# Soft-MoE attention kernel on one core: slot products on 64x32 tiles, compact key-value products, one bank for a pair's logits, a new order for phase 1

## The chip, the cores and the metric

One core of a Trainium2 chip runs the whole program in one launch. The metric is the device time of that launch in microseconds (us). The kernel before took 251.25 us, the median of 3 runs (250.69 to 259.25).

Engines are named as in the profile: PE (TensorE) multiplies matrices, and PEld is its loading of weights; DVE (VectorE) and ACT (ScalarE) do elementwise work and copy results out of PE's accumulator banks; POOL (GpSimd) does elementwise work on the memory the other engines share; SP (SyncE) issues the large transfers. Each engine works through its own list in order and waits for the others by semaphores.

## The reference: what is computed

Three stages follow one another. The program fuses them.

```python
# 1: attention, 8 batches x 8 heads x 576 positions x 64
q_s = softmax(q, over the 64)            # per position
k_s = softmax(k, over the 576 positions) # per column
kv  = einsum('bhsd,bhse->bhde', k_s, v)  # 64 x 64 per head
x   = einsum('bhsd,bhde->bhse', q_s, kv) # then 4608 tokens x 512
# 2: soft mixture of experts, 8 experts x 4 slots
logits = x @ phi                         # 4608 x 32
d = softmax(logits, over tokens);  slot_input = d.T @ x      # 32 x 512
slot_out = relu(slot_input[e] @ w1[e]) @ w2[e]               # 512 -> 1024 -> 512
y = softmax(logits, over slots) @ slot_out
# 3: top-1 mixture of experts on y, 8 experts, with gates
```

## The kernel before, in words

**Phase 1** covers stage 1 and the slot inputs of stage 2, and x is never formed. A unit u (0 to 7) is two batches (b = 0, 1) and four of their eight heads: 128 partitions by 2304 numbers each of q, of k and of v. Two units with the same batches make a pair (pr, 0 to 3). For each unit the steps are:

- `load_k`, `load_v`, `load_q` put transfers on SP's queue. `k_max` (DVE) and `k_exp` (ACT) make the exponentials of k; `k_t` transposes them on PE, four 128x128 blocks into one bank, and `k_te` copies the bank out (tile `ek`). `k_prod` (L256) multiplies them with v in 64x64 tiles of PE into the tile `kv`.
- `k_norm` copies `kv` into `kvbd`, a tile in which two 64x64 products stand as a block diagonal of a 128x128 block, the rest being zero. `k_kvT` (L287) transposes four such blocks, `k_kvTe` copies them out (ACT), `k_m` (L300) multiplies each with 32 columns of phi, and `k_mt` (DVE) scales the result: `mq`, which takes a position's 64 exponentials of q straight to its 32 logits.
- `q_max` (DVE), `q_sub` (POOL), `q_exp` (ACT), `q_sum` (DVE), `q_mul` (POOL) make the softmax of q (`eq`); `q_t` (L365) transposes it on PE and `q_te` copies it out (`eT`).
- `logits` (L385) multiplies `eT` by `mq` on 128x32 tiles, into two banks per pair, one for each b.

For each pair, `logits_cp`, `logits_t` and the `disp_` steps subtract a running maximum over the tokens and exponentiate the logits into `dz`. `slots_u` (L476) then forms sum over positions of dz times eq, nine matmuls of 256 columns per unit, each on one of two 128x64 tiles of PE (the even and the odd r); `dz` is held with zeros where position group and slot column belong to different b. `slots_e` copies the result out, `slots_t` (L493) adds the two tiles' parts and transposes, `slots_m` scales, `slots_p` (L511) multiplies by `kvbd`, and `slots_acc` adds it to the running slot inputs `acc`.

A matrix product of 32-bit numbers shows as two records each in the trace, a transpose as one. So nine matmuls of `slots_u` are 18 records.

**The order** of phase 1 is written out: a table `ORDER` of some 800 steps, replayed as the program is recorded, so that each engine's list has the table's order. `PAUSES` adds, behind some steps, matmuls on zeros (L605) that nobody reads. Three banks are shared in turn by all results named `tp` (transposes and small products), two by `kv`, two by `L`, one by `U`.

**The weights** of stage 2 (w1 and w2, 33.5 MB) come in 1 MB tiles. `load_w` 0 and 1 have buffers of their own and stand in `ORDER`; the next 19 take over buffers of phase 1 as those are released (`W_TAGS` names them), and eleven more (`W_NEXT`) go into the buffers of weights that were already used, each after its product on PE (L689, `expert_in`). Then come the second product (L733) and a tail of some 74 us that routes the tokens and writes the output; the change leaves it alone.

SP's transfers use eight completion semaphores in turn, shared with the first transfers that ACT issues (`phi`, and the two halves of `wgo`): the ninth transfer waits until the first has landed.

## Time and profile before

| | us |
|---|---|
| median of 3 runs | 251.25 (250.69 to 259.25) |
| the profiled execution, its own time | 250.71 |
| its span, first to last instruction | 248.8 |
| PE busy in the span | 216.6 (87%) |
| DVE, ACT, POOL busy | 152.2, 137.8, 92.7 |
| data moved by the transfers | 76.64 MB, 308 GB/s on average |

The span is 1.9 us shorter than the execution's time; what lies around it is the launch. Busy times are averages over stages with different limits, so they are read by stage: phase 1 ends near 140 us, the experts' weights are through at 175 us, and the tail ends the span.

### The profile page before, as it was taken

How to read it: one execution, taken by the hardware profiler on the slowest of the kernel's cores; microseconds unless marked ns; L12 is line 12 of the kernel's file. 1: busy time of each engine (PE TensorE's matmuls, PEld its weight loads, DVE VectorE, ACT ScalarE, POOL GpSimd, SP SyncE). 2: the span in 40 equal slices, each digit the busy share in tenths (PEclk: the TensorE clock that was granted, in tenths of full speed). 3: DMA queues.
4: the chain of work that ended last, by engine and by line, in shares of the span. 5: the costliest groups of instructions: out<-in, count | busy, mean ns of one | idle time of the engine just before them, and what ended most of it. 6: DMA issues, size and time to landing. Idle time of an engine off the chain costs nothing.

```text
span 248.8 us, 7197 instructions
## 1 busy us (share of the span) xinstructions
PE 216.6 (87%) x2976; PEld 154.5 (62%) x2976; DVE 152.2 (61%) x306; ACT 137.8 (55%) x314; POOL 92.7 (37%) x87
## 2 busy tenths in 40 slices
PE   0678789999999999878999899998999999999940
PEld 0557668777787678665966555332675653888830
DVE  2899788869798877662236571411643888756330
ACT  2879588877997968641533111211333285788640
POOL 5088495727944676506100107312001483100000
PEclk9999999999999999999999999999999999999985
DMA  7999998896899995997999989997079020088991
GB/s 240 411 333 412 407 412 329 322 420 258 323 419 406 420 344 182 366 415 277 310 418 354 351 324 420 419 414 317 3 256 391 31 84 1 4 360 353 379 385 52
DMA packets 18134, 76.64 MB, mean 308 GB/s; under 512 B 3376, under 2 KB 5680, under 8 KB 13360
## 3 DMA queue, kind: packets, MB, share of 16 engines
q1 hardware_dynamic: 16352, 75.50, 77.6%
q0 software_dynamic: 160, 0.52, 0.7%
q8 instruction: 25, 0.41, 0.7%
q10 hardware_dynamic: 1584, 0.10, 0.4%
q14 instruction: 13, 0.11, 0.1%
HBM read 66.68 MB, written 9.44 MB: 306 GB/s over the span
## 4 chain that ended last, share of the span: by engine, by line
PE 57%; DMA 24%; DVE 7%; ACT 4%; issue 3%; SPq 0%; POOL 0%; ACTq 0%; DVEq 0%
DMA vz<-in_moe_w_dram 9%; PE kv L256 6%; PE tp L365 6%; DMA wgo<-n_moe_w_output_gate_dram 6%; PE U L476 6%; PE tp L230 5%; DMA we<-in_moe_w_dram 5%; PE L L385 5%; PE kv L1520 4%; DMA qh<-in_q_dram 4%; PE L L1520 3%; PE U L1520 2%; PE kv L689 2%; PE tp L300 2%; PE tp L287 1%
## 5 line engine op out<-in xcount | busy, mean ns | idle before, releaser
L358 POOL TENSOR_TENSOR eq<-eq,qs 128x1280 f32<-128x1280 f32 (+1 forms) x16 | 33.6, 2117 | 30.5 <-DVE qs L354 30.5
L333 POOL TENSOR_TENSOR eq<-qh,qm 128x1280 f32<-128x1280 f32 (+1 forms) x16 | 33.5, 2116 | 16.9 <-DVE qm L320 15.6
L230 PE MATMUL tp<-ident,kh 128*128 128x128 f32 x144 | 23.7, 299 | 10.7 <-ACT kh L221 9.4
L256 PE MATMUL kv<-vz,ek 64*64 64x64 f32 x1152 | 24.2, 223 | 4.8 <-issue 4.1
L256 PEld LDWEIGHTS kv<-vz,ek 64*64 64x64 f32 x1152 | 20.0, 134 | 9.9 <-issue 8.9
L230 PEld LDWEIGHTS tp<-ident,kh 128*128 128x128 f32 x144 | 17.3, 153 | 14.1 <-issue 8.7
L221 ACT ACTIVATE kh<-kh,nm 128x576 f32<-128x576 f32 x32 | 24.8, 775 | 0.4 <-DVE nm L213 0.2
L213 DVE TENSOR_REDUCE nm<-kh 128x2 f32<-128x1152 f32 x16 | 21.4, 1338 | 4.5 <-DMA kh<-in_k_dram 4.5
L237 ACT COPY eT<-tp 128x512 f32<-128x512 f32 (+1 forms) x32 | 16.4, 534 | 11.5 <-PE tp L365 11.2
L320 DVE TENSOR_REDUCE qm<-qh 128x36 f32<-128x2304 f32 x8 | 20.4, 2545 | 2.6 <-DMA qh<-in_q_dram 2.6
L344 DVE TENSOR_REDUCE qs<-eq 128x20 f32<-128x1280 f32 (+1 forms) x16 | 21.4, 1337 | 0.0
L365 PE MATMUL tp<-ident,eq 128*128 128x128 f32 x144 | 20.8, 280 | 0.3 <-ACT eT L237 0.3
L339 ACT ACTIVATE eq<-eq 128x1280 f32<-128x1280 f32 (+1 forms) x16 | 18.5, 1164 | 1.9 <-POOL eq L333 1.9
L476 PE MATMUL U<-eq,dz 128*64 128x256 f32 x144 | 18.8, 384 | 0.1
L237 ACT COPY ek<-tp 128x512 f32<-128x512 f32 (+1 forms) x32 | 16.4, 534 | 3.6 <-PE tp L230 3.2
L365 PEld LDWEIGHTS tp<-ident,eq 128*128 128x128 f32 x144 | 15.7, 142 | 3.5 <-issue 2.5
L476 PEld LDWEIGHTS U<-eq,dz 128*64 128x64 f32 x144 | 10.9, 136 | 6.0 <-issue 0.7
L733 PE MATMUL U<-we,hte 128*32 128x512 f32 (+1 forms) x118 | 13.4, 572 | 0.9 <-DMA we<-in_moe_w_dram 0.5
L385 PE MATMUL L<-eT,mq 128*32 128x128 f32 (+1 forms) x256 | 11.7, 291 | 0.0
L689 PE MATMUL kv<-we,sTm 128*32 128x256 f32 x188 | 11.6, 381 | 0.1
L1520 PE MATMUL kv<-mst,hr 128*128 128x512 f32 (+1 forms) x32 | 11.3, 390 | 0.0
L859 ACT ACTIVATE ob<-kv,gates 128x512 f32<-128x512 f32 x11 | 7.5, 688 | 4.1 <-PE kv L1520 2.8
(326 smaller groups left out, 415.3 us busy)
## 6 DMA issues: line engine op xcount, KB each, us to landing
we<-in_moe_w_dram SPq DMA_DIRECT2D x24, 1024.0 KB, 8.3
kh<-in_k_dram SPq DMA_DIRECT2D x16, 576.0 KB, 8.9
qh<-in_q_dram SPq DMA_DIRECT2D x8, 1152.0 KB, 9.3
vz<-in_v_dram SPq DMA_DIRECT2D x16, 576.0 KB, 9.4
out_dram<-ob SPq DMA_DIRECT2D x11, 768.0 KB, 3.3
vz<-in_moe_w_dram SPq DMA_DIRECT2D x5, 1024.0 KB, 12.0
vz<-in_moe_w_dram SPq DMA_DIRECT2D x6, 512.0 KB, 6.1
w2q<-in_moe_w_dram SPq DMA_DIRECT2D x4, 512.0 KB, 8.1
```

The costliest lines, as they stand in the source:

```text
L213: nc.vector.tensor_reduce(out=st_["nm", u][:, c], in_=kview(u, c), op=ALU.max, axis=AX.XY, negate=True)
L221: nc.scalar.activation(out=x, in_=x, func=AF.Exp, bias=st_["nm", u][:, c, b:b + 1], accum_out=st_["kz", u][:, c, b:b + 1])
L230: nc.tensor.transpose(tp[:, n * P:(n + 1) * P], ks_[u][:, j * P:(j + 1) * P], ident)
L237: nc.scalar.copy(out=out, in_=in_)
L256: nc.tensor.matmul(kv[b][D * hh:D * hh + D, c * D:(c + 1) * D], ek[a, x], vt[a, x], start=(r == 0), stop=(r == RQ - 1))
L333: nc.gpsimd.tensor_tensor(out=q_part(st_["eq", u], i), in0=q_part(qs_[u], i), in1=q_row(st_["qm", u], i), op=ALU.subtract)
L344: nc.vector.tensor_reduce(out=st_["qs", u][:, QC[i]:QC[i + 1]], in_=q_part(st_["eq", u], i), op=ALU.add, axis=AX.X)
L358: nc.gpsimd.tensor_tensor(out=e, in0=e, in1=q_row(st_["qs", u], i), op=ALU.mult)
L365: nc.tensor.transpose(tp[:, n * P:(n + 1) * P], eq[:, j * P:(j + 1) * P], ident)
L385: nc.tensor.matmul(lg[b][NS * g:NS * g + NS, :n * 64].rearrange("p (i t) -> p i t", t=64), mq[:, 2 * c + b, :], ev[:, c, g:RQ:4, 64 * b:64 ...
L476: nc.tensor.matmul(U[64 * (r % 2):64 * (r % 2) + 64, hf * HH * D:(hf + 1) * HH * D], dz[:, r].rearrange("p b s -> p (b s)"), eq[:, r * HH ...
L1520: nc.tensor.matmul(op, a[:, x], w[:, d0:d1], start=(k == 0), stop=(k == 2))
```

## The change

Six things are changed, all in phase 1 but the last.

1. `slots_u` uses 64x32 tiles, eight of them (two groups b, four places g = r mod 4), so 18 matmuls of 256 columns per unit instead of nine. `dz` loses its zeros and halves in size; the results go to two banks (`L`), copied out by ACT and by DVE, and `slots_t` does eight matmuls instead of four.
2. The block diagonal `kvbd` becomes `kvc`, 64x64 products side by side. `k_norm` copies once instead of twice per b, `k_kvT` transposes two blocks instead of four, `k_m` does eight 64x64 matmuls instead of four of 128x128, into two `tp` banks instead of one, and `k_mt` and `slots_p` follow. `phi` is loaded twice, once for each half of the partitions.
3. The logits of a pair share the one bank `U`; a matmul of zeros opens it.
4. `disp_new` and `disp_al` compute the rescaling factor with other small instructions.
5. `ORDER` and `PAUSES` are new. `load_w.0` moves to the end of phase 1's loads.
6. The two zeroed tiles `sTm` of the expert stage lie in one tile, that of `slots_e`.

```diff
 PAUSES = {
-    "k_te2.0": 1, "q_sub0.1": 32, "load_k1.2": 1, "logits_cp1.3": 3, "logits_out.3": 3, "slots_e.2": 4,
-    "disp_al.3": 3, "slots_m.3": 3, "slots_t.3": 0,
+    "k_te0.0": 2, "k_max0.2": 4, "k_t3.1": 8, "disp_max.3": 5, "logits_out.3": 7, "slots_m.3": 5, "slots_t.3": 0,
 }
...
 ORDER = """
-load_k0.0 k_max0.0 k_exp0.0 k_exp1.0 load_k1.0 load_k0.1 k_max1.0 k_exp2.0 k_t1.0 k_exp3.0 k_t0.0 k_max0.1 load_q.0
...
+load_k0.0 k_max0.0 load_k0.1 k_exp0.0 load_k1.0 k_max0.1 load_q.0 k_exp1.0 k_max1.0 k_exp0.1 k_exp3.0 k_t1.0 k_exp2.0
...
     def k_norm(u, b):
         pr, hf = halves(u)
-        for hh in range(2):
-            a = slice(D * hh, D * hh + D)
-            copy_to(
-                b == 1, kvbd[pr % 2][a, b, 2 * hf:2 * hf + 2, a],
-                st_["kv", u][b][a, :2 * D].rearrange("p (c x) -> p c x", c=2),
-            )
+        copy_to(
+            b == 1, kvc[pr % 2][:, 2 * hf:2 * hf + 2, b, :],
+            st_["kv", u][b][:, :2 * D].rearrange("p (c x) -> p c x", c=2),
+        )
...
     def k_kvT(u):
         for c in range(2):
-            for b in range(2):
-                j = 2 * c + b
-                nc.tensor.transpose(tk[:, j * P:(j + 1) * P], bd[:, b, 2 * hf + c, :], ident)
+            nc.tensor.transpose(
+                tk[:, c * P:(c + 1) * P], kvc[pr % 2][:, 2 * hf + c].rearrange("p b x -> p (b x)"), ident
+            )
...
     def k_m(u):
-        mp = bank("tp")
-        for j in range(4):
-            nc.tensor.matmul(
-                mp[:, NS * j:NS * j + NS], kvT[:, j, :], phi_sb[:, 2 * hf + j // 2, :], start=True, stop=True
-            )
+        mp = [bank("tp") for _ in range(2)]
+        for c in range(2):
+            for hh in range(2):
+                for b in range(2):
+                    a = slice(64 * b, 64 * b + 64)
+                    nc.tensor.matmul(
+                        mp[b][D * hh:D * hh + D, NS * c:NS * c + NS], kvT[a, c, D * hh:D * hh + D],
+                        phi2[a, HH * hf + 2 * c + hh, :], start=True, stop=True,
+                    )
...
     def logits(u):
         if hf == 0:
-            st_["L", pr] = [bank("L") for _ in range(2)]
+            lg = st_["L", pr] = bank("U")
+            nc.tensor.matmul(lg[:, :6 * D], zero[:, :P], zero, start=True, stop=False)
...
     def disp_exp(pr):
-        for b in range(2):
-            nc.scalar.activation(out=dz[64 * b:64 * b + 64, :, b, :], in_=dl[64 * b:64 * b + 64], func=AF.Exp)
+        nc.scalar.activation(out=dz_t[pr % 2], in_=st_.pop(("dl", pr)), func=AF.Exp)
...
     def slots_u(pr, hf):
         for r in range(RQ):
-            nc.tensor.matmul(
-                U[64 * (r % 2):64 * (r % 2) + 64, hf * HH * D:(hf + 1) * HH * D],
-                dz[:, r].rearrange("p b s -> p (b s)"),
-                eq[:, r * HH * D:(r + 1) * HH * D],
-                start=(r < 2),
-                stop=(r >= RQ - 2),
-            )
+            g = r % 4
+            for b in range(2):
+                a = slice(64 * b, 64 * b + 64)
+                nc.tensor.matmul(
+                    U[b][NS * g:NS * g + NS, hf * HH * D:(hf + 1) * HH * D], dz[a, r],
+                    eq[a, r * HH * D:(r + 1) * HH * D], start=(r < 4), stop=(r >= RQ - 4),
+                )
...
-    def slots_e(pr):
-        U_sb = sp.tile([P, H * D], F32, tag="U_sb", name="U_sb")
-        nc.scalar.copy(out=U_sb, in_=st_.pop(("U", pr)))
-        st_["Us", pr] = U_sb
+    def slots_e(pr, b):
+        if b == 0:
+            st_["Us", pr] = sp.tile([P, 2, H * D], F32, tag="U_sb", name="U_sb")
+        copy_to(b == 1, st_["Us", pr][:, b], st_["U", pr][b])
 
     def slots_t(pr):
         for c in range(C):
-            nc.tensor.matmul(tu[:, c * 64:c * 64 + 64], U_sb[:, c * P:(c + 1) * P], sum2, start=True, stop=True)
+            for b in range(2):
+                j = 2 * c + b
+                nc.tensor.matmul(
+                    tu[:, j * NS:j * NS + NS], U_sb[:, b, c * P:(c + 1) * P], sum4[:, 0, :], start=True, stop=True
+                )
...
-    W_TAGS = "x x z00 k z01 q k q ek z10 k ek z11 A eq eq eT eT eq eq B".split()
+    W_TAGS = "x x z00 k z01 k q q ek z10 k ek z11 A eq eq eT eT eq eq B".split()
...
-    nc.scalar.dma_start(out=phi_sb, in_=phi.rearrange("(c p) s -> p c s", p=P))
+    for b in range(2):
+        nc.scalar.dma_start(out=phi2[D * b:D * b + D], in_=phi.rearrange("(h d) s -> d h s", d=D))
```

Where the table puts the slot products, on PE, at the first pair (`slots_u0.0` and `slots_u1.0`; L230 and L223 are `k_t`, L365 and L362 are `q_t`, L256 and L249 are `k_prod`). Before:

```order
L448 MATMUL tp<-ident,m_new 128x32
L300 MATMUL tp<-phi_sb,kvT 128x32 x4
L230 MATMUL tp<-ident,kh 128x128 x4
L365 MATMUL tp<-ident,eq 128x128 x8
L476 MATMUL U<-eq,dz_98 64x256 x9
L256 MATMUL kv<-vz_100,ek 64x64 x16
L230 MATMUL tp<-ident,kh 128x128 x2
L287 MATMUL tp<-ident,kvbd_101 128x128 x4
L256 MATMUL kv<-vz_100,ek 64x64 x16
```

And in the change:

```order
L454 MATMUL tp<-ident,m_run 128x32
L362 MATMUL tp<-ident,eq 128x128 x4
L223 MATMUL tp<-ident,kh 128x128 x4
L362 MATMUL tp<-ident,eq 128x128 x4
L276 MATMUL tp<-ident,kvc_97 128x128 x2
L249 MATMUL kv<-vz_96,ek 64x64 x16
L223 MATMUL tp<-ident,kh 128x128 x2
L483 MATMUL L<-eq,dz_95 32x256 x18
L362 MATMUL tp<-ident,eq 128x128 x2
```

The slot products keep their place among transposes and key-value products; the small products `k_m` move off from between the running maximum (L448, L454) and the slot products.

The first loads on SP with what each waits for, from the sixth on, before (L192 is `load_k`, L196 `load_v`, L201 `load_q`):

```order
L201 DMA qh<-in_q_dram 128x2304 [waits DMAHW0_49]
L192 DMA kh<-in_k_dram 128x1152 [waits DMAHW1_49]
L196 DMA vz_100<-in_v_dram 128x1152 [waits DMAHW2_49]
L196 DMA vz_100<-in_v_dram 128x1152 [waits DMAHW3_49]
L196 DMA vz_100<-in_v_dram 128x1152 [waits DMAHW4_49]
L196 DMA vz_100<-in_v_dram 128x1152 [waits DMAHW5_49]
L201 DMA qh<-in_q_dram 128x2304 [waits DMAHW6_49,DVE_49,Pool_49]
```

And in the change (L185, L189, L194 are the same three loads), from the fifth on:

```order
L185 DMA kh<-in_k_dram 128x1152 [waits DMAHW0_49]
L185 DMA kh<-in_k_dram 128x1152 [waits DMAHW1_49]
L194 DMA qh<-in_q_dram 128x2304 [waits DMAHW2_49]
L189 DMA vz_96<-in_v_dram 128x1152 [waits DMAHW3_49]
L189 DMA vz_96<-in_v_dram 128x1152 [waits DMAHW4_49]
L185 DMA kh<-in_k_dram 128x1152 [waits DMAHW5_49]
L189 DMA vz_96<-in_v_dram 128x1152 [waits DMAHW6_49]
L189 DMA vz_96<-in_v_dram 128x1152 [waits DMAHW7_49]
L185 DMA kh<-in_k_dram 128x1152 [waits DVE_49,DMAHW0_49,PE_49,Activation_49]
L194 DMA qh<-in_q_dram 128x2304 [waits DMAHW1_49,DVE_49,Pool_49]
```

Here semaphores 0 and 2 are those of the two `phi` transfers, 3 and 5 those of the two halves of `wgo`: the second q load waits for the second `phi`, the first v load for the first half of `wgo`. Before, semaphore 0 was that of `phi`, 2 and 3 those of `wgo`: the second q load waited for `phi`, the first v load for the first half of `wgo`, which had one small transfer less ahead of it. The third q load (the last row of each) moves from behind four v loads to behind four v and three k loads.

## Rows read from the trace of the kernel before

**Rows 1.** The page, busy time by engine: us (share) x instructions.

```profile
PE 216.6 (87%) x2976; PEld 154.5 (62%) x2976; DVE 152.2 (61%) x306; ACT 137.8 (55%) x314; POOL 92.7 (37%) x87
```

**Rows 2.** Busy time by stage: length, engines' busy us, granted clock, transfer share, GB/s.

```profile
34.00:124.00 90.00, 84.73 (x1590) 67.52 (x1592) 65.59 (x103) 65.73 (x155) 51.15 (x26) 1.00 0.90 345
124.00:140.20 16.20, 14.31 (x195) 9.75 (x188) 7.48 (x18) 4.29 (x11) 1.02 (x4) 1.00 0.95 384
140.20:175.00 34.80, 33.60 (x415) 14.63 (x417) 12.36 (x33) 5.73 (x18) 9.01 (x22) 1.00 0.91 363
175.00:248.80 73.80, 62.81 (x398) 45.02 (x394) 41.05 (x126) 38.43 (x83) 11.75 (x18) 0.95 0.51 194
```

**Rows 3.** The chain that ended last, in order of time: start, length, what.

```profile
18.35 9.20 DMA qh<-in_q_dram
27.65 2.55 DVE qm L320
...
34.86 0.87 PE tp L230 x6
...
38.36 1.02 PE tp L365 x8
39.38 0.62 PE kv L256 x32
...
42.46 0.81 PE tp L300 x8
...
50.65 0.59 PE tp L287 x4
51.24 1.09 PE kv L256 x64
...
56.18 2.30 PE U L476 x18
...
66.61 0.92 PE tp L493 x8
...
70.92 0.56 PE tp L511 x14
...
140.16 5.43 PE kv L689 x96
145.61 11.58 DMA we<-in_moe_w_dram
157.25 17.43 DMA vz<-in_moe_w_dram
```

**Rows 4.** What PE waited for from 34 to 124 us: total, times, longest.

```profile
PE kv L256 <- issue: 2.3, 2, 1.9
PE tp L230 <- ACT ek L237: 0.7, 1, 0.7
```

**Rows 5.** Groups by line and shape: busy us, mean ns, idle before.

```profile
L235 DVE COPY eT<-tp 128x512 f32<-128x512 f32 x8 | 5.5, 689 | 6.6 <-PE tp L365 6.5
```

**Rows 6.** The end of phase 1 as a timeline: start, length, engine, line.

```profile
126.35 0.51 PE L605 MATMUL tp<-zero 128*128 128x264 bf16 x3
...
129.93 0.89 ACT L462 ACTIVATE dz<-dl 64x288 f32<-64x288 f32 x2 [0.99 <-DVE dl L455]
...
130.86 1.14 DVE L466 TENSOR_REDUCE ds<-dz 128x32 f32<-128x576 f32 x1 [0.96 <-ACT dz L462]
130.88 4.53 PE L476 MATMUL U<-eq,dz 128*64 128x256 f32 x36
...
134.74 1.17 ACT L592 ACTIVATE l_all<-l_all 128x1152 f32<-128x1152 f32 x1 [3.92 <-DVE l_all L591]
```

**Rows 7.** What SP's queue waited for: total, times, longest.

```profile
SPq L196 <- DMA wgo<-in_moe_w_gate_dram: 8.0, 1, 8.0
...
SPq L196 <- DMA wgo<-n_moe_w_output_gate_dram: 2.9, 1, 2.9
```

**Rows 8.** SP's issues as a timeline: start, length, what.

```profile
142.89 6.08 SPq L552 DMA_DIRECT2D we<-in_moe_w_dram  x7
```

## The prediction

> **What bounds the kernel now.** I read the page first: PE is the busiest engine [rows 1], but an average over the span says little. So the windows by stage came next. From 34 to 124 us PE is busy 84.73 of 90 us, DVE and ACT 65.6 and 65.7, POOL 51.15, and the transfers take 0.90 of their time [rows 2]. The chain of waits names PE in nearly every piece of that stretch; the pieces shown stand for the others [rows 3]. Third, the waits of PE there: the largest is 2.3 us that the profile cannot put down to anything, the next 0.7 us on a copy [rows 4]. So from 34 to 124 us the bound is PE's own work, and DVE and ACT have about 24 us of slack each. Before 34 us the chain runs over the loads and DVE (the q load of 9.20 us that starts at 18.35, then its maximum of 2.55 us [rows 3]). From 124 to 140.2 us it is a string of short dependent steps. From 145.6 to 174.7 us the chain holds two long pieces of weight transfers, 11.58 and 17.43 us [rows 3], with the transfers at 0.91 and 363 GB/s [rows 2]. The tail of 73.8 us is untouched.

> Durations come from the profiled execution, whose own time is 250.71 us; the median of the three runs is 0.54 us above it, and I add that at the end.

> **How PE's groups are priced.** A group of 32 records of key-value products takes 0.62 us, one of 64 takes 1.09 [rows 3]: 0.47 us for 32 more records, so 14.7 ns each, and 0.15 us per group for getting in. Each of the other rows holds such an entry, too.

> **The change, part by part (PE, 34 to 124 us).**
> - *Slot products.* Nine matmuls take 2.30 us [rows 3]. Five of them share one of the two tiles, so one matmul costs (2.30 - 0.15) / 5 = 0.43 us on its tile, when the tiles run side by side. With eight tiles and 18 matmuls the fullest tile has three (r = 0, 4, 8): 3 x 0.43 + 0.15 = 1.44 us, a saving of 0.86. Three of four pairs lie in this stretch, six groups: **-5.2 us**. This holds if eight 64x32 tiles run together, which no row shows. The nearest rows are four 64x64 tiles (14.7 ns per record where one tile needs 0.43 us x 64/256 / 2 = 54 ns, so 3.6 wide) and four 128x32 tiles, 96 records in 5.43 us or 57 ns each [rows 3], where one tile alone needs 215 (half of 0.43), so 3.8 wide. If only four ran together, 18 matmuls cost 18/4 x 0.43 + 0.15 = 2.1 us, and the saving were 0.2 per group, 1.2 us in all. I take eight, since both rows get nearly all that their tiling allows in rows or in columns, and the new one only combines them.
> - *k_m.* Four products take 0.81 us [rows 3]. The new ones are 16 records in 64x64 tiles, at 14.7 ns 0.24 us; entering that tiling costs 0.15, leaving it another 0.15 unless a key-value group stands beside it. I take 0.39, so -0.42 (between -0.27 and -0.57). Seven of eight lie here: **-2.9 us**.
> - *k_kvT.* Four transposes take 0.59 us [rows 3], eight 1.02 [rows 3], so 0.11 each: two fewer save 0.22, seven times: **-1.5 us**.
> - *slots_t.* Eight records take 0.92 us [rows 3]; twice as many with weights of the same size, less one entry, add 0.75. Two pairs here: **+1.5 us**.
> - *slots_p.* 0.56 us [rows 3] becomes 32 records at 14.7 ns and an entry or two, 0.62 to 0.77: **+0.3 us** for two pairs.
> - *The zero matmul of logits.* Three dummies of 264 columns take 0.51 us [rows 6]; one of 384 columns and an entry is at most 0.25 + 0.15, I take 0.25, four times: **+1.0 us**.

> The sum is -5.2 - 2.9 - 1.5 + 1.5 + 0.3 + 1.0 = **-6.8 us**.

> [...]

> **Other engines.** ACT loses one of two copies per `k_norm`, half of each `k_kvTe`, one exponential per pair: all gain, hidden by its slack. DVE gets four copies of 128x512 (689 ns [rows 5]) in `slots_e`, a second small product in each `k_mt`, and loses a copy per unit and half of `disp_sum` (1.14 us [rows 6]): about even. If PE needs 6.8 us less, DVE's 65.6 us lie in 83 us, 79%: still cover. POOL loses clearings before its first q work, which waited for DVE anyway.

> **The end of phase 1 (124 to 140.2 us).** The second of two `dz` exponentials goes (0.89 becomes 0.45), `disp_sum` halves (-0.6, estimated from its 1.14 [rows 6]), `slots_t` adds 0.75, `slots_p` and the third accumulation some 0.3. The last pair's slot products (4.53 us for both halves [rows 6]) get shorter but gain nothing: the copy behind them also waits for ACT's exponential of all logits, which starts at 134.74 [rows 6], when they are nearly through. Net **0**. The two clearings of `sTm` come after `slots_t` now, beside `slots_m`, `slots_p` and the accumulation.

> **The start.** SP sat 8.0 us before its first v load, until a small transfer of ACT had landed [rows 7]. Now one more of these stands ahead of that one, and the second q load waits for it. Bounds: 0, if the transfers stay busy meanwhile with the loads ahead, and some 3 us, the wait for the next such transfer, 2.9 us [rows 7]. The chain of 18 to 34 us hangs on the third q load, which moves behind three k loads. I take **+0.5**, near the lower end, because k loads fill the gap.

> **Banks.** `k_m` and `slots_p` now take two of the three `tp` banks. PE waited 0.7 us for the copies of k's transposes [rows 4] and less for others; a bank less for a moment exposes at most a copy (0.69 us [rows 5]) twelve times, 8 us. As the groups before are mostly already copied, I take 0.1 for eight of them: **+0.8**.

> **Load_w.0** moves from among the q loads to the end of phase 1's loads. The same bytes go through, the transfers have 9 us idle in this stretch (below), and its product comes only at 140 us: nothing.

> **Does it reach the end?** The first weights that replace used ones are issued at 142.89 [rows 8], when the first product is done, and eleven of them set the end of the weights at 174.7. A phase 1 that ends earlier moves them as far, if what is ahead of them has been transferred. From 34 to 124 us the transfers had 10% idle, 9 us, and that idle was for buffers that PE releases. So I let the shift through whole, as the upper bound; nothing as the lower (the rival below).

> -6.8 + 0 + 0.5 + 0.8 = -5.5: 250.71 - 5.5 = 245.2, and against the median **245.7 us**. Its own range, from the bounds of the parts, is 243 to 248.5.

> **Rivals.**
> 1. *The weights become the bound.* PE gets done earlier, but the transfers do not: at 345 GB/s average in the stretch and 384 behind it [rows 2] they have little room, as the one weight tile is later too. Then at most 1 to 2 us arrive at the end: 249.5. For it: 0.95 and 0.91 busy behind 124 us [rows 2]. Against it: 9 us idle before.
> 2. *Banks or the start cost more*, 3 to 5 us of the bounds above: 249 to 250. For it: the ring of three is tight; against it: rows 4.
> 3. *The new order also takes idle time out.* PE stands 5.3 us in the main stretch [rows 2], and PE starts its dense part only at 34.86 [rows 3]; if 4 to 5 us of that go: 241.
> 4. *The slot tiles do not run together (slower).* With two at a time a group costs 18/2 x 0.43 + 0.15 = 4.0 us, +1.7 instead of -0.86. Six groups add 10.2 - the other parts' -1.6 = +8.6, with the last pair's 3.4 partly exposed and 1.3 of start and banks: 262. It decides from 2.97 us per group on (2% of 251 is 5 us over eight groups). [...] For it: no row of eight tiles; against it: both rows of four.

> **Chances.** Forecast 0.48; rival 1 0.18; rival 2 0.10; rival 3 0.15; rival 4 0.05; a loss that I did not see 0.04. About 2% (5 us) is what a measurement of this kernel can tell from no change. Faster than 246.2: two thirds of the forecast and nearly all of rival 3, **0.47**. Slower than 256.3: rival 4, the unseen and a tenth of rivals 1 and 2, **0.12**. The rest, **0.41**, is within 2%. The range that leaves out rival 4 and the best of rival 3 is **241 to 252**.

> **What would show it.** The group of 36 records of slot products at 1.4 us each (2.1: four wide; 4.0: two wide). `k_m` groups near 0.4, `k_kvT` near 0.37, `slots_t` near 1.7. The first records of L689's counterpart near 134 us instead of 140.16, and the last weight 5 to 6 us before 174.7. If the former moves and the latter does not, rival 1 is right. PE waits on copies of `tp` above 3 us mean rival 2. A first dense stretch of PE later than 34 us means that the start was underpriced. The forecast is wrong if the tail, 73.8 us, changes as well.

## The result, and the profile after

The changed kernel takes **248.39 us** (median of 4 runs, 246.75 to 249.38) against 251.97 us for the kernel before (4 runs, 250.69 to 259.25): ratio 0.9864, 95% interval [0.9815, 0.9913]. A second comparison, made with later experiments, gave 249.1 us and 0.980 [0.968, 0.992]. The forecast was 245.7 us with a range of 241 to 252. So the direction and the range hold; of the forecast's 5.5 us some 3.4 came by the ratio, and the median lies 2.7 us above the forecast. What the forecast held likeliest (chance 0.47, a gain of more than 2%) did not come in the first comparison: the gain is under 2%, to which it gave 0.41. The ratios, and comparisons drawn from them, leave out disturbed runs and the medians do not; two profiles below (old_slots, late_warm) are of disturbed runs and are used for the order of events alone.

The profiled execution of after took 248.17 us (span 246.2) against 250.71 (span 248.8) before. PE's row of the page, to be held against [rows 1]:

```profile
PE 210.8 (86%) x3249; PEld 147.8 (60%) x3249; DVE 150.2 (61%) x309; ACT 132.5 (54%) x298; POOL 90.0 (37%) x83
```

PE is busy 5.8 us less, yet the span is only 2.6 us shorter. Note the count: 273 records more (a record is one weight load with its matmul). The stages of [rows 2] end earlier now, so the stretch from 34 us to the end of the last logits matmul is the better yardstick. Before (columns as in [rows 2]: length, then busy time of PE, PEld, DVE, ACT and POOL, granted clock, transfer share, GB/s):

```profile
34.00:126.40 92.40, 87.13 (x1641) 69.25 (x1640) 65.59 (x103) 66.32 (x157) 51.15 (x26) 1.00 0.90 346
```

and after, with the two stages behind it:

```profile
34.00:123.00 89.00, 81.93 (x1864) 62.88 (x1862) 63.96 (x104) 62.93 (x143) 53.03 (x26) 1.00 0.91 354
123.00:136.90 13.90, 11.65 (x216) 8.42 (x216) 8.30 (x21) 3.04 (x7) 1.48 (x5) 1.00 1.00 416
136.90:173.90 37.00, 34.65 (x418) 14.67 (x419) 12.36 (x33) 5.79 (x18) 9.01 (x22) 1.00 0.89 349
```

The stretch is 3.4 us shorter. PE works 5.2 us less in it and stands 7.1 us instead of 5.3. What it waited for (the counterpart of [rows 4]: total, times, longest):

```profile
PE kv L249 <- issue: 4.2, 3, 1.6
PE U L383 <- issue: 1.9, 2, 1.6
PE L L483 <- issue: 0.7, 1, 0.7
```

The wait on a copy in [rows 4] is gone. In its place stand 6.8 us of "issue", time in which PE waited for nothing that the profile shows, against 3.1 us before. [rows 4] shows two of the five waits of before; the prediction's "the next 0.7 us on a copy" passes over two that are longer:

```profile
PE tp L404 <- DVE lT L235: 1.0, 1, 1.0
PE tp L404 <- issue: 0.8, 1, 0.8
```

The chain of after shows such a stop in the middle of a run of equal matmuls, and the new groups (start, length, what; the counterpart of [rows 3]):

```profile
25.50 1.44 issue
...
35.55 0.66 PE tp L223 x4
...
43.13 1.09 PE U L383 x22
44.23 1.56 issue
45.79 0.51 PE U L383 x7
...
56.86 1.31 issue
...
58.98 1.42 PE L L483 x36
...
68.69 1.71 PE tp L499 x16
...
73.04 0.38 PE tp L521 x32
...
136.92 5.48 PE kv L700 x97
...
155.41 17.37 DMA vz<-in_moe_w_dram
```

The slot group takes 1.42 us. The group of 29 logits records at 43.13 is cut after 22 of them, 1.56 us long. `expert_in` starts at 136.92 instead of 140.16, and the last weight lands at 172.78 (155.41 + 17.37) instead of 174.68.

PE's groups in the stretch, by line, before (matmuls alone: busy us, mean ns, idle before):

```profile
L256 PE MATMUL kv<-vz,ek 64*64 64x64 f32 x864 | 18.4, 224 | 2.3 <-issue 2.3
L476 PE MATMUL U<-eq,dz 128*64 128x256 f32 x108 | 14.2, 385 | 0.0
L300 PE MATMUL tp<-phi_sb,kvT 128*128 128x32 f32 x56 | 7.0, 270 | 0.0
L287 PE MATMUL tp<-ident,kvbd 128*128 128x128 f32 x28 | 4.4, 280 | 0.0
L493 PE MATMUL tp<-sum,U_sb 128*128 128x64 f32 x16 | 2.1, 273 | 0.0
L511 PE MATMUL tp<-kvbd,UT 128*32 128x128 f32 x32 | 1.3, 279 | 0.0
```

and their counterparts after:

```profile
L249 PE MATMUL kv<-vz,ek 64*64 64x64 f32 x864 | 19.3, 224 | 4.2 <-issue 4.2
L483 PE MATMUL L<-eq,dz 64*32 64x256 f32 x216 | 9.2, 382 | 0.7 <-issue 0.7
L294 PE MATMUL tp<-phi,kvT 64*64 64x32 f32 x128 | 3.8, 222 | 0.0
L499 PE MATMUL tp<-sum,U_sb 128*128 128x32 f32 x32 | 3.7, 271 | 0.0
L276 PE MATMUL tp<-ident,kvc 128*128 128x128 f32 x14 | 2.9, 287 | 0.0
L375 PE MATMUL U<-zero 128*128 128x384 bf16 x4 | 1.3, 334 | 0.0
L521 PE MATMUL tp<-kvc,UT 64*32 64x64 f32 x64 | 0.9, 222 | 0.0
```

The mean of one record hardly changes from 385 to 382 ns in the slot products, while twice the records take 9.2 instead of 14.2 us: more of them run side by side. The gain of packing shows here in the busy time per record, not in the mean.

### The profile page after: what moved, and what is told of

Its sections match the earlier page's. It is cut to its first block, busy times and chain, and to the rows that moved or that the text cites. A ratio compares the mean times of both kernels' runs of the same rounds, so it can differ in the third digit from the quotient of the medians.

```text
span 246.2 us, 7722 instructions
## 1 busy us (share of the span) xinstructions
PE 210.8 (86%) x3249; PEld 147.8 (60%) x3249; DVE 150.2 (61%) x309; ACT 132.5 (54%) x298; POOL 90.0 (37%) x83
## 4 chain that ended last, share of the span: by engine, by line
PE 63%; DMA 21%; issue 4%; DVE 3%; ACT 3%; ACTq 1%; SPq 0%; POOL 0%; DVEq 0%
PE kv L249 8%; PE tp L362 8%; DMA vz<-in_moe_w_dram 7%; PE tp L223 6%; DMA we<-in_moe_w_dram 5%; DMA wgo<-in_moe_w_gate_dram 5%; PE U L383 5%; PE kv L1531 4%; DMA vz<-in_v_dram 4%; PE L L483 4%; PE L L1531 3%; PE kv L700 2%; PE U L1531 2%; PE tp L499 2%; PE tp L276 1%
## 5 line engine op out<-in xcount | busy, mean ns | idle before, releaser
L223 PE MATMUL tp<-ident,kh 128*128 128x128 f32 x144 | 25.0, 314 | 9.9 <-ACT kh L214 8.9
L249 PE MATMUL kv<-vz,ek 64*64 64x64 f32 x1152 | 25.8, 227 | 7.7 <-issue 5.7
L249 PEld LDWEIGHTS kv<-vz,ek 64*64 64x64 f32 x1152 | 21.0, 137 | 12.8 <-issue 9.7
L223 PEld LDWEIGHTS tp<-ident,kh 128*128 128x128 f32 x144 | 18.4, 159 | 14.2 <-issue 9.6
L362 PE MATMUL tp<-ident,eq 128*128 128x128 f32 x144 | 21.8, 284 | 0.0
L230 ACT COPY eT<-tp 128x512 f32<-128x512 f32 (+1 forms) x32 | 16.4, 537 | 6.9 <-PE tp L362 6.7
L230 ACT COPY ek<-tp 128x512 f32<-128x512 f32 (+1 forms) x32 | 16.6, 531 | 6.6 <-PE tp L223 6.3
L336 ACT ACTIVATE eq<-eq 128x1280 f32<-128x1280 f32 (+1 forms) x16 | 18.4, 1171 | 1.1 <-POOL eq L330 1.1
L362 PEld LDWEIGHTS tp<-ident,eq 128*128 128x128 f32 x144 | 15.9, 143 | 2.5 <-issue 1.0
L383 PE MATMUL U<-eT,mq 128*32 128x128 f32 (+1 forms) x256 | 12.1, 291 | 1.9 <-issue 1.9
L483 PE MATMUL L<-eq,dz 64*32 64x256 f32 x288 | 11.9, 382 | 0.7 <-issue 0.7
L383 PEld LDWEIGHTS U<-eT,mq 128*32 128x32 f32 x256 | 8.0, 109 | 4.6 <-issue 3.7
```

Source lines behind the costliest of these rows:

```text
L223: nc.tensor.transpose(tp[:, n * P:(n + 1) * P], ks_[u][:, j * P:(j + 1) * P], ident)
L230: nc.scalar.copy(out=out, in_=in_)
L249: nc.tensor.matmul(kv[b][D * hh:D * hh + D, c * D:(c + 1) * D], ek[a, x], vt[a, x], start=(r == 0), stop=(r == RQ - 1))
L362: nc.tensor.transpose(tp[:, n * P:(n + 1) * P], eq[:, j * P:(j + 1) * P], ident)
L383: nc.tensor.matmul(lg[NS * g:NS * g + NS, b, :n * 64].rearrange("p (i t) -> p i t", t=64), mq[:, c, b, :], ev[:, c, g:RQ:4, 64 * b:64 * b ...
L483: nc.tensor.matmul(U[b][NS * g:NS * g + NS, hf * HH * D:(hf + 1) * HH * D], dz[a, r], eq[a, r * HH * D:(r + 1) * HH * D], start=(r < 4), s ...
```

## The experiments

Three questions: what the new operations and the new order are worth apart, what the stops are, and whether the start can be mended. One table for all, each kernel from its own profile. "Busy", "idle" and "issue" are PE's, from 34 us to the end of the last logits matmul; "records" are the matmuls in it; each ratio is to the kernel before as run beside that kernel; "half" is the time there at a granted clock of 0.5.

| kernel | median us | ratio to before | logits end | busy | idle | issue | half | records |
|---|---|---|---|---|---|---|---|---|
| before | 251.97 | 1 | 126.4 | 87.1 | 5.3 | 3.1 | 0 | 1641 |
| after | 248.39 | 0.986 [0.982, 0.991] | 123.0 | 81.9 | 7.1 | 6.8 | 0 | 1864 |
| after_again | 249.10 | 0.980 [0.968, 0.992] | 122.2 | 81.8 | 6.4 | 6.3 | 0 | 1860 |
| order_old_ops | 254.75 | 1.015 [1.003, 1.026] | 127.0 | 89.6 | 3.4 | 2.6 | 0 | 1643 |
| ops_old_order | 263.82 | 1.056 [1.047, 1.065] | 135.6 | 89.4 | 12.2 | 6.2 | 13.7 | 1896 |
| old_slots | 253.57 | 1.011 [1.001, 1.021] | 133.1 | 91.4 | 7.7 | 7.0 | 13.7 | 1741 |
| old_kv | 249.25 | 0.996 [0.988, 1.003] | 124.1 | 86.3 | 3.8 | 3.7 | 0 | 1773 |
| warm_start | 252.60 | 0.997 [0.991, 1.003] | 124.7 | 83.4 | 7.3 | 6.5 | 3.4 | 1880 |
| small_late | 248.93 | 0.987 [0.978, 0.995] | 122.8 | 82.5 | 6.3 | 6.0 | 0.6 | 1864 |
| late_warm | 251.47 | 0.999 [0.995, 1.004] | 126.0 | 84.1 | 7.9 | 7.8 | 3.4 | 1883 |
| few_big | 253.48 | 1.016 [1.006, 1.025] | 127.7 | 92.4 | 1.3 | 1.0 | 0 | 1905 |
| many_small | 264.88 | not given | 140.0 | 100.9 | 5.1 | 5.1 | 17.0 | 2334 |
| shift48 | 254.53 | 1.002 [0.996, 1.009] | 129.0 | 87.3 | 7.7 | 7.6 | 9.4 | 1893 |
| wide_kv | see there | | 114.2 | 79.0 | 1.2 | 0 | 0 | 1424 |

**after_again** is the changed kernel itself, run once more beside the next three.

> The changed kernel once more, as the measure for the three beside it: 247 to 249.5 us.

Measured: 249.1 us, as expected. Its stops come behind the same counts of records as those of after, with two more of 0.5 us (behind 347 and 1742).

**order_old_ops: the new order alone.**

```diff
 # before, with the tables ORDER, PAUSES and W_TAGS of after
-slots_e0.0 ... slots_e1.0
+slots_e.0
```

> The operations of the kernel before under the new order and pauses. Theory: no gain from the order, 250.5 to 253 us, PE as busy in phase 1 as before. Rival, the order makes the gain: 248 to 249. Rival, the order costs (its start: the first clock drop and the second q load behind a small transfer): 253 or more.

```profile
34.00:127.00 93.00, 89.59 (x1643) 70.14 (x1642) 65.87 (x101) 67.01 (x155) 52.49 (x26) 1.00 0.90 347
```

Measured: 254.75 us, slower than before by 0.3 to 2.6%; the theory's 250.5 to 253 is missed, and the rival that the order costs gave 253 or more. Against before the stretch holds 2.5 us more of PE's work and 1.9 us less idle; the logits end 0.6 us later. The order brings nothing by itself. The records are as many (1643 for 1641), but the key-value products take 19.3 us where the same 864 took 18.4, in 25 groups instead of 22:

```profile
L255 PE MATMUL kv<-vz,ek 64*64 64x64 f32 x864 | 19.3, 224 | 2.7 <-issue 2.6
```

Transposes of q take 19.7 us for 132 records instead of 18.0 for 126, `k_m` 8.2 for 61 instead of 7.0 for 56, transposes of k 14.1 for 94 instead of 15.9 for 102. At the prices of before these shifts in number come to about 0.2 us (an estimate from these lines), so most of the 2.5 us is like work that takes longer, and not work left over from the start; why it takes longer was not settled. How much of the loss in time is the order's stays open: the two profiles' spans differ by 4.1 us, of which 2.5 lie in the tail, whose program is the same. Against after, which shares its order, it gives the operations' own worth: 89.6 - 81.9 = **7.7 us of work**.

**ops_old_order: the new operations alone.**

```diff
 # after, with the tables ORDER and PAUSES of before
-slots_e.0
+slots_e0.0 slots_e1.0
```

> The new operations under the order and pauses of the kernel before (each copy-out of slot products is followed by its second half). Theory: the gain comes from the operations. PE's work in phase 1 falls by about 6.7 us, and part of it comes back as idle time that the profile calls issue, because PE runs through its instructions faster than they are brought in (the trace of the changed kernel shows 6.8 us of it from 34 to 124 us, that of before 3.1). So 247 to 249.5 us, with 5 to 8 us of issue idle in phase 1. Rival, the banks: products that take two of three shared banks stall PE where the order was not made for them; then 251 or more, with PE waiting for copies by ACT and DVE. Rival, the order: if the new order makes the gain, this one stays at 251 to 253.

Measured: 263.82 us, 12 us slower than before. The theory (247 to 249.5) is refuted; the rival of the banks said 251 or more with waits on copies, and these came, but no theory expected the size. Two windows of its profile (columns as above), and what PE waited for in the whole stretch:

```profile
66.70:70.10 3.40, 1.42 (x23) 1.03 (x21) 3.40 (x3) 3.40 (x8) 2.09 (x2) 1.00 1.02 416
70.10:73.50 3.40, 3.19 (x15) 3.19 (x16) 0.98 (x4) 0.09 (x1) 3.40 (x2) 0.50 1.00 415
```

```profile
PE tp L500 <- DVE eT L229: 1.6, 1, 1.6
PE tp L295 <- ACT eT L231: 1.6, 2, 0.9
```

`k_m` (L295) and `slots_t` (L500) wait for copies out of the `tp` banks; all waits on such copies come to some 5 us in the stretch. In the first window PE is busy 1.42 of 3.40 us, and in the next 3.40 us the granted clock is 0.50; three times in the stretch it falls to that level, for 13.7 us in all. So the banks' price is real, but in an order that was not made for two banks a product; in the new order those waits are gone.

**old_slots and old_kv: one half of the operations undone.**

```diff
 # old_slots: after, with before's dz, disp_exp, disp_sum, slots_u, slots_e, slots_t
-for b in range(2): nc.tensor.matmul(U[b][NS*g:NS*g+NS, ...], dz[a, r], eq[a, ...], ...)
+nc.tensor.matmul(U[64*(r%2):64*(r%2)+64, ...], dz[:, r].rearrange("p b s -> p (b s)"), eq[:, ...], ...)
 # old_kv: after, with before's k_norm, k_kvT, k_kvTe, k_m, k_mt, slots_p, slots_acc
-kvc.append(at.tile([P, C, 2, D], F32, name=f"kvc{i}"))
+t = at.tile([P, 2, C, P], F32, name=f"kvbd{i}")
+nc.gpsimd.memset(t, 0.0)
```

> The changed kernel with the slot products back on two 128x64 tiles (9 matmuls, dz with zeros, one copy-out, four products in slots_t); all else and the order stay. Theory: six groups cost 0.88 us more each, slots_t of two pairs 0.8 less each, so PE has 3.7 us more work on its path; 72 fewer matmuls are 288 fewer instructions, about one stop for instructions (1.3 to 1.6 us) less. So 2 to 3 us above the changed kernel, 250 to 251.5. Rival, the tiles' gain is hidden: no more than 0.5 us above.

Measured: 253.57 us, above the expected 250 to 251.5. The rival falls: without the new slot products nothing is left of the gain. The size is inconclusive: 13.7 us of the profiled stretch ran at half the clock.

> The changed kernel with the block-diagonal key-value products back (k_norm with four copies, four transposes, four products in one bank, slots_p by the block diagonal, phi loaded once); slot products, the bank for logits and the order stay. Theory: 2.9 + 1.5 us more on PE's path, 0.3 less in slots_p, one stop for instructions less, so 2 to 3.5 us above the changed kernel, 250 to 252. Rival, the banks: since the two-bank products go, PE stalls less, and it is within 1 us of the changed kernel.

```profile
34.00:124.10 90.10, 86.30 (x1773) 68.32 (x1772) 64.86 (x100) 65.91 (x149) 52.14 (x25) 1.00 0.90 351
```

Measured: 249.25 us, under the expected 250 to 252. The medians put it 0.9 us above after, the ratios about 2 us, and their intervals overlap, so the time alone does not settle theory against rival. The profile says more: PE's work grows by 4.4 us, as the forecast's terms for `k_m` and `k_kvT` say (2.9 + 1.5). But the idle time falls by 3.3 us, since 3.1 us of issue stops go, and the logits end only 1.1 us later. Of the key-value half's 4.4 us three quarters are given back as stops. The rival's number came near, its mechanism did not: after has no waits on banks that could go.

**warm_start, small_late, late_warm: the start.** The theory was that the first dense stretch suffers from the clock or from the small transfers in front of v.

```diff
 # warm_start: more dummy matmuls
-"k_te0.0": 2, "k_max0.2": 4, "k_t3.1": 8,
+"k_te0.0": 8, "k_max0.2": 12, "k_t3.1": 20,
 # small_late: the loads of phi2 issued behind k_te2.0, those of wgo behind disp_exp.0
 # late_warm: both
```

> The changed kernel with 26 more matmuls on zeros in the gaps of PE before 20.5 us (8, 12 and 20 instead of 2, 4 and 8 at the first three places of PAUSES). In the changed kernel the granted clock came to its full level at 17.2 us instead of 12.5 and fell back to half from 27.4 to 30.8. Theory of the start: the half clock makes PE late by 1 to 2 us of work at 34 us; with the gaps filled the clock is full earlier and does not fall, and the time drops by 0.5 to 2 us. Rival, the loads set the start: the clock changes and the time does not (within 0.5 us).

Measured: 252.6 us, by the ratios some 4 us slower than after_again, although the granted clock came to its full level at 11.7 us instead of 15.2. Neither expectation came. The theory of the clock at the start falls: after_again, too, had no fall of the clock at 27 us, as after had (0.50 from 27.4 to 30.8 us), and its profiled execution is only 0.9 us shorter (247.32 against 248.17). Why this kernel is slower is open; about half of it lies ahead of the logits' end, the rest in the tail.

> The changed kernel with ACT's four small transfers issued later (the two of phi after k_te2.0, the two of wgo after disp_exp.0), so that no early load on SP's queue waits for their semaphores. In the changed kernel the second q load was issued at 12.9 us behind phi and the first v load at 14.4 behind wgo, before at 4.9 and 13.7. Theory, the loads set the start: first v product by 3 to 5 us earlier, time lower by 1 to 3 us. Rival, the clock or DVE sets the start: the loads come earlier and the time stays within 0.5 us.

Measured: 248.93 us, the same as after_again within the noise. The first v product came earlier, at 18.4 us instead of 20.5, which is 2.1 us and not 3 to 5; but the third q load landed at 31.9 us in both. The small transfers do not set the time.

> Both edits. If loads and clock each bind, 2 to 4 us under the changed kernel; if only one does, as that one alone.

Measured: 251.47 us, not under the changed kernel but above it: again the warm start's loss.

**few_big and many_small: the same PE time in few or in many instructions.**

```diff
         ops[n](int(i))
+        if op in (...):             # k_prod2.u and q_t1.u, u = 1 to 7
+            scratch = bank("tp")
+            for x in range(5):      # many_small: 32 of 8 columns
+                nc.tensor.matmul(scratch[:32, :384], zero[:, :32], zero[:, :384], start=True, stop=True)
```

> The same places with 5 matmuls of 384 columns on zeros instead: 140 more instructions, some 0.8 to 0.95 us of PE time at each place. Both theories: 11 to 13 us more of PE work, so 257 to 262 us; by the theory of instructions the issue idle is as in the changed kernel (7 us from 34 us to the last logits) or less, since PE stays longer with each instruction.

> The changed kernel with 32 matmuls of 8 columns on zeros (32 weights each) behind 14 steps of phase 1 (k_prod2 and q_t1 of units 1 to 7): 896 more instructions for PE, some 0.8 us of PE time at each place. Theory, PE runs out of instructions: against the kernel with few big ones at the same places (756 instructions fewer) it has 3 to 5 us more idle time that the profile calls issue, and is 2 to 5 us slower. Rival, the issue idle comes from changing between tilings: both make the same number of changes, and the idle is alike within 1 us.

Measured: few_big 253.48 us, under the 257 to 262 that both theories gave; many_small 264.88 us, 11 us above it instead of 2 to 5. The added records in few_big, then in many_small:

```profile
L629 PE MATMUL tp<-zero 128*32 128x384 bf16 x70 | 14.0, 328 | 0.2 <-ACT eT L230 0.2
```

```profile
L629 PE MATMUL tp<-zero 128*32 128x8 bf16 x448 | 13.8, 167 | 3.7 <-issue 3.7
```

Both add the same time to PE. With the long records the stops all but vanish (issue 1.0 us instead of 6.8). Of the 14.0 us added 13.0 lie in the stretch; PE's work there grows by 10.5 us, its idle time falls by 5.8, and the logits' end moves by only 4.7, so the time stays under its forecast. With the short ones 5.1 us of issue stay, 4.1 more than in few_big, as the theory of instructions said (3 to 5; its rival said alike within 1). But 17 us run at half the clock, which costs some 8 us (an estimate, half of the 17; PE is busy 8.5 us longer than in few_big, 100.9 against 92.4) and is most of its loss; a slower PE also needs its instructions later, so its stops are not a clean measure. What few_big shows is clean: long records take the stops away.

**shift48: where the stops are.**

```diff
+        if op in ("k_te0.0", "k_t3.1"):
+            scratch = bank("tp")
+            for _ in range(24):
+                nc.tensor.matmul(scratch[:32, :8], zero[:, :32], zero[:, :8], start=True, stop=True)
```

> Adds 48 matmuls of 8 columns on zeros, 24 behind k_te0.0 and 24 behind k_t3.1, both before 21 us, where PE stands idle. Theory (instructions come in pieces, so the stops lie at fixed counts of records from the start): PE stops again behind about 220, 601, 854, 1361, 1488 and 1996 records, which are now 48 records earlier in the program: the stop inside the first logits group (L383, 22 of 29 records) and the one inside a slot group (L483) are gone, and stops come inside key-value groups ahead of them. The time stays within 2 us of 248.4, since only the records at a stop change. Rival (the stops belong to what the program does there: a change of tile, a bank, a copy): the stops stay in the same groups, behind 649, 902, 1409, 1536 and 2044 records.

Windows from the span's start to a stop count the records ahead of it. After, to its stops at 44.23, 56.86, 80.07 and 108.12:

```profile
0.00:44.23 44.23, 30.83 (x601) 25.05 (x601) 34.01 (x39) 32.06 (x74) 22.98 (x17) 0.96 0.98 372
0.00:56.86 56.86, 41.77 (x854) 33.60 (x854) 43.69 (x53) 41.75 (x94) 31.19 (x21) 0.97 0.98 382
0.00:80.07 80.07, 63.67 (x1361) 50.41 (x1362) 63.00 (x81) 59.65 (x133) 46.74 (x28) 0.98 0.95 369
0.00:108.12 108.12, 89.42 (x1996) 70.58 (x1996) 84.45 (x117) 79.30 (x177) 63.94 (x37) 0.98 0.93 364
```

and shift48, to four of its own:

```profile
0.00:44.22 44.22, 30.65 (x601) 25.57 (x601) 31.63 (x37) 29.83 (x66) 21.62 (x16) 0.92 0.97 376
0.00:63.88 63.88, 48.33 (x981) 38.81 (x982) 46.58 (x56) 43.11 (x97) 33.79 (x22) 0.92 0.96 374
0.00:90.19 90.19, 72.22 (x1488) 57.49 (x1488) 65.83 (x90) 62.64 (x140) 47.32 (x29) 0.92 0.91 356
0.00:113.22 113.22, 93.80 (x1996) 74.51 (x1996) 84.30 (x117) 79.94 (x177) 63.47 (x36) 0.94 0.88 342
```

The first of these stops comes behind 601 records in both, and 601 again in warm_start, which has 26 records more ahead of it:

```profile
0.00:43.22 43.22, 29.09 (x601) 23.33 (x601) 32.38 (x38) 30.44 (x68) 21.64 (x16) 1.00 0.95 367
```

The 48 records moved the stop to another place in the program: in shift48's chain it cuts a key-value group, and the first logits group behind it runs through.

```profile
43.60 0.62 PE kv L249 x31
44.22 1.98 issue
46.20 0.50 PE kv L249 x17
...
48.38 2.34 PE U L383 x29
```

All differences are multiples of 126 to 127 records: 854 - 601 = 253, 1361 - 854 = 507, 1996 - 1361 = 635, 981 - 601 = 380. This decides between the theories: what stops PE is neither a tile, nor a bank, nor a copy, but the count of instructions since the start. Of the six stops expected, those behind 221, 601, 1488 and 1996 records came, that behind 1361 was short (0.53 us), and that behind 854 did not come; one of 1.9 us behind 981 came in its place, and 0.9 us of issue behind 348 follow a wait for ACT. All lie on the same grid, but not every boundary stops PE. The other kernels agree, the one before among them, whose stops come behind 220, 346, 727, 1360 and 1867 records: in the traces of the table there are 66 stops for issue of 0.4 us or more between 20 and 135 us, and all 66 lie within three records of 220 plus a whole multiple of 126.85. The time, 254.5 us, missed its expectation of within 2 us of 248.4: 9.4 us of the stretch ran at half the clock, and the stops grew to 2.0 us. Why the clock fell here more than in after stays open.

**wide_kv: the same columns through PE in half the key-value records.**

```diff
-for j in range(4 * i, min(4 * i + 4, 2 * RQ)):
+for j in range(4 * i, min(4 * i + 4, 2 * RQ), 2):
...
-    kv[b][D*hh:D*hh+D, c*D:(c+1)*D], ek[a, x], vt[a, x], ...
+    kv[b][D*hh:D*hh+D, c*P:(c+1)*P], ek[a, x:x+D], vt[a, x:x+P], ...
```

> Changed computation: a key-value record now takes 128 columns of v instead of 64 and the record of the next block is left out, so 576 records stand for 1152 and PE streams as many columns as before; the sums are no longer those of the reference. From 34 us to the last logits matmul about 1435 records remain of 1864. Theory (PE runs out of instructions, which come in pieces of some 127 records): busy PE stays near 82 us, the idle time called issue falls from 6.8 us to 2 or less, the logits end near 118 to 119 instead of 123.0, and with half of it lost to the weights as before the time is 245 to 246.5. Rival (the stops belong to changes of tiling or to places in the program, not to the number of records): idle stays at 6 to 7 us and the time at 248.4.

```profile
34.00:114.20 80.20, 79.00 (x1424) 58.46 (x1423) 63.98 (x104) 62.30 (x142) 53.25 (x26) 1.00 1.00 398
```

The changed sums send the experts into the kernel's loop for overfull ones (L1630), so its total of 476.6 us says nothing; phase 1 and the weights are read alone. There PE works 79.0 us, stands 1.2 us, and not once for "issue". The logits end at 114.2, 8.8 us before those of after and further ahead than expected, and `expert_in` starts at 128.3. The theory holds: with fewer records the stops go. The rival (idle stays at 6 to 7 us) falls.

## Why the prediction was right, and where it was short

**The price of the operations** was right. By line, after less before in the stretch, against the forecast: slot products 9.2 - 14.2 = -5.0 (-5.2); `k_m` 3.8 - 7.0 = -3.2, though it holds eight units instead of seven, so at 0.475 a unit -3.7 for seven (-2.9); `k_kvT` -1.5 (-1.5); `slots_t` +1.6 (+1.5); `slots_p` -0.4 (+0.3; it runs on 64x32 tiles and was priced on 64x64); the zero matmul +1.3 (+1.0). Together -7.7, the same as the experiment with equal order, against -6.8. The group of 36 records takes 1.42 us where 1.44 was forecast: eight 64x32 tiles run together. Rival 4 (two at a time, 4.0 us per group by the forecast's sum) is refuted: its width was a supposition that no run shows, and the trace has 1.42 us.

**The order** was underpriced: +0.5 was taken, for its start alone and within bounds of 0 to 3, and nothing for what it does to PE's work. With operations unchanged, the new order has 2.5 us more work behind 34 us (order_old_ops), 1.0 us of it in the same 864 key-value records, and most of it not work left over from the start. (The table holds 526 steps before and 530 after, not some 800.) The sign that the prediction named, a dense start later than 34 us, shows less: in the chain it starts at 35.55 instead of 34.86. Mending the start's transfers or its clock did not help, and none of the experiments ends below the changed kernel; small_late equals it.

**The banks** were the wrong mechanism: +0.8 was taken for `tp` waits. Waits on copies fell from 2.0 us in the stretch (three rows, the longest of them for the logits' copy and not for a `tp` bank) to nothing. The order did this: with the old operations under it (order_old_ops) PE waits 0.6 us for other engines, with the new operations under the old order some 5 us for copies. What grew in their place is the time called issue, 3.1 to 6.8 us. The prediction had that row before it, the largest of [rows 4], 2.3 us, and put it aside as something the profile cannot explain; it priced the 273 added records by their PE time alone.

The sum at the logits' end is then -7.7 (operations) + 2.5 (order) - 2.0 (copies) + 3.7 (stops) = **-3.5**, where the windows say 3.4 and the forecast had -5.5. Its errors offset each other in part: the operations are 0.9 us better than forecast and the copies 2.8, the order 2.0 worse and the stops 3.7. So the direction was right by the price of the operations, and the size came as near as it did partly by luck.

**The end of phase 1** was right at nothing: `expert_in` starts 3.24 us earlier, the logits end 3.4 earlier.

**The shift passing through whole** failed in part: the first weights are issued 2.8 us earlier,

```profile
140.08 5.65 SPq L562 DMA_DIRECT2D we<-in_moe_w_dram  x7
```

against 142.89 [rows 8], but the last weight comes only 1.9 us earlier. That looks like rival 1, yet it is not shown to be it: in wide_kv `expert_in` starts 8.6 us before that of after, and `expert_out`, which waits for the last weight, ends 8.9 us before, so far larger shifts pass. From the start of `expert_in` to that end the kernels take 34.8 to 37.1 us (before 35.6, after 37.0), and 1.3 us lie within that spread; earlier starts lean to the longer times, but from wide_kv to many_small the start moves by 25.8 us and the end by 24.0.

The tail got 0.7 us shorter (246.2 - 172.78 against 248.8 - 174.68), and 1.9 + 0.7 is the 2.6 us of the span. The prediction held the tail fixed and named a change of it as a sign of being wrong. Its program is the same; before, the chain waits there for a weight transfer, and after it does not:

```profile
182.23 5.62 DMA vz<-in_moe_w_dram
```

Between the kernels of the table, wide_kv aside, the time from the end of `expert_out` to the end of the span varies from 72.3 to 75.5 us, so 0.7 us is nothing that the change can be credited with. By the ratio the gain is 3.4 us, by the two spans 2.6; runs of one kernel vary by more than what is left.

The measured 248.4 and 249.1 us are near rival 2's times (249 to 250), but its mechanism did not come. Rival 3 is half there: waits on copies went as it says, and were outweighed.

## What to carry to other kernels

Count PE's instructions as well as their time: here, with products packed into more and smaller tiles, PE's work in the stretch was 5.2 us less and its stops for instructions were 3.7 us more. A row of "issue" that cuts a run of equal matmuls is the sign; count the records ahead of each such stop, and if the counts agree between kernels and differ by multiples of a constant, as here by multiples of 126.85 records, no wait or bank is to blame. An order that was made for one set of operations is part of their price: either half of this change, run without the other, was slower than the kernel before.

## What the runs showed of the hardware

**PE's instructions arrive in pieces.** The page of after counts them as a queue of their own (packets, MB, share):

```profile
q8 instruction: 27, 0.44, 0.7%
```

**A lull was followed by a slow stretch.** In ops_old_order PE stood 2.0 us of the 3.40 us up to 70.10, and in the next 3.40 us the granted clock was 0.50 and 15 matmul records took 3.19 us. Old_slots aside, the three kernels of the table with over 9 us of the stretch at that level (shift48, ops_old_order, many_small) are the three whose logits end last, at 129.0, 135.6 and 140.0 us.
